# Block 1's rows as SyncE's first load, and its raw transposes ahead of V of block 0

## The chip, the cores and the metric

The kernel runs on one core of a Trainium2 chip. The metric is the device time of one execution in microseconds (us). Before the change the median of three runs is 236.48 us (236.21 to 236.73).

## What is computed

Two branches work on the same normalised input of 2048 rows by 512 columns, and are added to it: A is an attention of 32 heads over a sliding, dilated window of 8 positions, B is a gated MLP in which the positions are mixed by a 2048 by 2048 matrix.

```python
xn = layernorm(x)                              # x: [2048, 512]
# A: q, k, v = xn @ wqkv; 32 heads of 16; window of 8 positions, step 2
q, k, v = split(xn @ wqkv)
attn = softmax(mask(q . k[s - 2*w], w = 0..7) * 16**-0.5)
A = (sum_w attn[w] * v[s - 2*w]) @ wo
# B: gated MLP, gate mixed over the positions
z = gelu(xn @ w_in)                            # [2048, 1792]
z1, z2 = z[:, :896], layernorm(z[:, 896:])
B = (z1 * (w_sp @ z2 + b_sp[:, None])) @ w_out
out = x + A + B
```

## The kernel before

The 2048 rows are worked on in 16 blocks of 128 rows and 4 groups of 512. All inputs are bfloat16. For a matmul the rows of x must lie along the free dimension, so each block is transposed. Blocks 1 to 15 are normalised on VectorE and then transposed by a DMA that SyncE issues (`xTd1` and so on, L640). Block 0's normalised rows are transposed on TensorE instead (`xTr0`).

V, the product of x with the last third of `wqkv`, is wanted early to give TensorE work. For blocks 0 to 2 (`NRAW = 3`) it is therefore computed from raw rows, before the layernorm's statistics are known, and mended later (L754). These raw rows are transposed on TensorE as products with an identity (`pe_tr`, L600): block 0 in two tasks of two 128-column matmuls each (`xTx0a`, `xTx0b`), blocks 1 and 2 in one task of four (`xTx1`, `xTx2`). ScalarE copies the result out of PSUM (L628): for blocks 0 and 1 in two halves (`xTc0_0`, `xTc0_1`, `xTc1_0`, `xTc1_1`), for block 2 in one piece. V of a block is two tasks of two 512-column matmuls (L700): `V0_0` takes the first half of the transposed block and of V's weights (`ldwv0`), `V0_1` the second half of both (`ldwv1`). Then come `z2` (L831, x with the second half of `w_in`), Q and K (L723), `z1` (L877), the mixing matmul (L977), and the output (L1033, L1042).

Until the first rows have landed TensorE runs warm-up matmuls on a constant (L581): `warm0` to `warm5` with 512 columns, `warm6` with 128, and one more of 128 columns, `warm7`, between block 0's transposes and V.

Order. Each operation is a task with the tiles that it reads and writes. A planner (`Plan.schedule`) places the tasks by estimated durations and so fixes the order on every engine and the PSUM bank of every product; `emit` then writes the instructions in this order with the semaphore waits that the tiles ask for. A bank that is handed out again makes its new user wait for the old one's readers. Two things are given to the planner by hand: lists of names that must follow one another (L1073 to L1083), among them TensorE's order of the first 11 us, and the landing times of the early loads (`land`, L1089), in ns. In the planner's order SyncE issues its loads in the order of the program text: V's weights in two halves, then rows of blocks 2 and 3, `w_in`'s second half in two parts, and rows of block 4. The rows of blocks 0 and 1 are issued by ScalarE.

What orders work around the change:

- ScalarE's queue: the loads of blocks 0 and 1, then a table load and one activation (L585), then `xTc0_0`.
- SyncE's queue: the loads above, then from `xTd1` on DMA transposes, which wait for VectorE's normalised blocks.
- VectorE: statistics of block 0 (`bnst0`, L620), small operations, statistics of block 1, and so on, in a list by hand.
- TensorE: the list by hand.

Of the kernel before, what the change touches and what calls it, by code (L numbers as in the profile page):

```python
# [346 lines left out]
def build_kernel(nc, A_x, A_wqkv, A_wo, B_x, B_w_in, B_w_sp, B_b_sp, B_w_out, out, report=False, emit=True):  # L347
# [13 lines left out]
    NWARM = 7  # L361
# [49 lines left out]
    with ExitStack() as es:  # L411
# [5 lines left out]
        def A(name, n, o2_=0):  # L417
            return ar[:, off[name] + o2_: off[name] + o2_ + n]
# [13 lines left out]
        def P(bk, n, o_=0):  # L432
            return ps[:, bk.col(o_): bk.col(o_) + n]
# [78 lines left out]
        def dma(eng, fn, nbytes, chan, reads=(), writes=(), name="", xbar=False, prio=0.0, after=()):  # L512
            return T(eng, fn, reads=reads, writes=writes, name=name, prio=prio, after=after,
                     dma=dict(chan=chan, nbytes=nbytes, xbar=xbar, iss=(1270.0 if nbytes < 400000 else 2200.0) if xbar else None))
# [18 lines left out]
        def ld_x(b, eng="sp"):  # L533
            sl = b
            return dma(eng, lambda e: e.dma_start(A("xin", 512, 512 * sl), x2[128 * b:128 * b + 128, :]), 128 * 512 * 2,
                ("xin", sl), writes=[("xin", sl)], name="ldx%d" % b)

        def ld_wv(hf):
            dma("sp", lambda e: e.dma_start(AC(off["wv"] + 1024 * hf, [[512, 2], [1, 512]]),
                                            A_wqkv[256 * hf:256 * hf + 256, 1024:1536].rearrange("(c p) n -> p c n",  # L540
                                                                                               p=128)),
                256 * 512 * 2, ("wv", hf), writes=[("wv", hf)], name="ldwv%d" % hf)
# [13 lines left out]
        def ld_wqk(which, eng):  # L556
# [4 lines left out]

        dma("act", lambda e: e.dma_start(A("xin", 512), x2[0:128, :]), 128 * 512 * 2, ("xin", 0),
            writes=[("xin0", 0), ("xin0", 1)], name="ldx0")
        ld_x(1, "act")
        ld_wv(0)
        ld_wv(1)
        ld_x(2, "sp")
# [8 lines left out]
        ld_wqk(1, "sp")  # L576

        bw = plan.bank("warm")
        for wi in range(NWARM + 1):
            n_ = 512 if wi < 6 else 128  # L580
            T("pe", (lambda bw, n_: lambda t: t.matmul(P(bw, n_), ones[:, 0:128], ones[:, 0:n_], start=True,  # L581
                                                       stop=True))(bw, n_),
              writes=[bw], est=(427.0 if n_ == 512 else 107.0), name="warm%d" % wi, prio=1000)
# [487 lines left out]

        byname = {t.name: t for t in plan.tasks}
        for names in (["warm%d" % wi for wi in range(NWARM)] +  # L1073
                      ["xTx0a", "xTx0b", "warm%d" % NWARM, "V0_0", "xTx1", "V0_1", "xTx2", "V1_0", "V1_1", "xTr0", "V2_0", "V2_1",
                       "z2_0_0", "z2_0_0b", "z2_0_1", "z2_1_0", "z2_1_1", "z2_2_0", "z2_2_1", "V3_0", "V3_1", "z2_3_0", "z2_3_1", "V4_0", "V4_1", "z2_4_0", "z2_4_1", "Q0_0", "Q0_1", "K0_0", "K0_1"],
                      ("rstd7", "Vw3"),
                      ("bnst0", "bnag0", "vpe0", "bnst1", "bnag1", "vpe1", "norm0", "bnst2", "norm1", "bnag2", "vpe2", "bnst3", "norm2",
                       "bnag3", "vpe3", "norm3", "bnst4", "bnag4", "vpe4", "mr", "norm4", "bnst5"),
                      ["bnst%d" % b for b in range(5, NB)],
                      ("xTc0_0", "xTc0_1", "xTc1_0", "xTc1_1", "xTc2_0", "xTe0_0", "xTe0_2", "Ve1", "Ve0", "Ve2",  # L1080
                       "z2g0", "z2g1", "z2s0"), ("ldx4", "xTd1", "xTd2", "xTd3", "xTd4", "ldq", "ldk", "ldx5", "ldx6", "ldx7", "ldwin1", "ldx8"), ("ldx15", "xTd5"),
                      *[("ldwin1", "ldx%d" % b) for b in range(9, NB)], *[("z2_4_1", "%s0_%d" % (n, c)) for n in "QK" for c in range(4)],
                      ("V10_1", "Q3_3"), ("csa", "csb", "csc", "csr", "ldwout"), ("csr", "ldwo0"), ("csr", "ldxr0"), ("csv", "zr3")):  # L1083
            for n0, n1 in zip(names, names[1:]):
                if byname[n0] not in byname[n1].deps:
                    byname[n1].odeps.add(byname[n0])

        plan.schedule(tol=4.0, dma_bw=285.0, dma_lat=1600.0, overlap=60.0,
                      land=dict(ldx0=3600.0, ldwv0=4120.0, ldx1=4550.0, ldwv1=5230.0, ldx2=5600.0, ldwin2a=7650.0, ldx3=6050.0,  # L1089
                                ldwin2b=8950.0, csa=75800.0, csb=78400.0, csc=83400.0, csr=86500.0, ldx4=9100.0, ldx5=18150.0, ldq=16300.0, xTd3=12130.0, ldk=17800.0, ldx6=18500.0, ldx7=18900.0, xTd4=13900.0, xTd1=9600.0, xTd2=10850.0, ldwin1=21500.0))  # L1090
        if report:
            print("arena", AR, "fp", FR)
# [17 lines left out]
def bass_parallel_sum__sliding_local_dilated__mixer_gmlp__prompt_kernel(  # L1110
    nc, A_x, A_wqkv, A_wo, B_x, B_w_in, B_w_sp, B_b_sp, B_w_out, out
):
    build_kernel(nc, A_x, A_wqkv, A_wo, B_x, B_w_in, B_w_sp, B_b_sp, B_w_out, out)
# [28 lines left out]
```

## Time and profile before

| | us |
|---|---|
| median of 3 runs | 236.48 (236.21 to 236.73) |
| the profiled execution | 236.54 |
| its span in the profile | 235.3 |
| VectorE busy | 207.3 (88%) |
| ScalarE busy | 95.9 (41%) |
| GpSimd busy | 29.4 (12%) |

The span is the time from the program's first instruction to its last on the core; some 1.2 us of the execution lie around it. Times inside the profile count from the span's start. A matmul's row in the profile shows it from its start to the modelled end of its last result, and the next one starts before that end, so the distance of two starts tells the rate. Weight loads (PEld) run beside the matmuls. The chain of waits is followed back from the last instruction: at each step to what released it, or to the instruction before it on its engine.

### The profile page before, as it was taken

The page shows a single profiled execution, that of the slowest core. Times are in us where ns is not written, and L with a number is a line of the kernel's source. Part 1 is how long each engine was busy: PE and PEld are TensorE (multiplying, and loading weights), DVE is VectorE, ACT ScalarE, POOL GpSimd, SP SyncE. Part 2 cuts the span into 40 slices and gives each one's busy share as a digit, 9 for nine tenths or more (in the row PEclk, how much of TensorE's full clock was granted, in tenths as well). Part 3 has the DMA queues.
Part 4 walks back from the last instruction along what each step waited for, and adds up shares of the span by engine and source line. Part 5 has one row for each costly group of instructions (what it writes and reads, how often), then busy time and mean ns, then how long its engine had stood idle before and what let it go on. Part 6 is the DMA issues. An engine that isn't in the chain of part 4 may idle for free.

```text
span 235.3 us, 3002 instructions
## 1 busy us (share of the span) xinstructions
PE 232.4 (99%) x1127; PEld 109.0 (46%) x1127; DVE 207.3 (88%) x271; ACT 95.9 (41%) x143; POOL 29.4 (12%) x58
## 2 busy tenths in 40 slices
PE   8999999999999999999999999999999999999996
PEld 3545445544454444444444444444444444444443
DVE  4706899999999999999899999998899998999723
ACT  3788878888986679610120531111111111000000
POOL 2305740404361202000000000000000000000000
PEclk9999999999999999999999999999999999999999
DMA  6669934999911285346199999999969849945442
GB/s 221 203 193 368 181 68 103 215 202 214 228 45 50 67 231 173 66 94 175 58 353 239 273 212 266 195 236 288 279 180 306 269 145 303 288 115 156 111 137 68
DMA packets 83991, 44.55 MB, mean 189 GB/s; under 512 B 56180, under 2 KB 83204, under 8 KB 83976
## 3 DMA queue, kind: packets, MB, share of 16 engines
q1 hardware_dynamic: 82744, 41.94, 69.6%
q0 software_dynamic: 800, 2.11, 3.0%
q10 hardware_dynamic: 432, 0.30, 0.4%
q8 instruction: 9, 0.15, 0.3%
q14 instruction: 6, 0.05, 0.1%
HBM read 26.62 MB, written 4.22 MB: 131 GB/s over the span
## 4 chain that ended last, share of the span: by engine, by line
PE 98%; DVE 0%; ACT 0%; issue 0%; DVEq 0%
PE ps L977 41%; PE ps L723 12%; PE ps L831 10%; PE ps L877 10%; PE ps L1042 10%; PE ps L700 6%; PE ps L1033 6%; PE ps L581 1%; PE ps L767 1%; PE ps L600 1%; DVE arena L1048 0%; ACT arena L628 0%; PE ps L778 0%; DVEq L325 0%
## 5 line engine op out<-in xcount | busy, mean ns | idle before, releaser
L977 PE MATMUL ps<-arena 128*128 128x512 bf16 x448 | 97.0, 379 | 0.0
L977 PEld LDWEIGHTS ps<-arena 128*128 128x128 bf16 x448 | 43.8, 98 | 53.0 <-issue 0.4
L985 ACT ACTIVATE arena<-ps 128x1024 bf16<-128x1024 f32 (+1 forms) x16 | 14.7, 917 | 77.0 <-PE ps L977 70.6
L1005 DVE TENSOR_TENSOR arena<-arena 128x4096 bf16<-128x4096 bf16 x16 | 36.4, 2282 | 0.0
L744 DVE TENSOR_TENSOR arena<-arena 128x4096 bf16<-128x4096 bf16 x16 | 36.4, 2280 | 0.0
L1008 DVE TENSOR_TENSOR arena<-arena 128x2048 bf16<-128x2048 bf16 (+1 forms) x32 | 30.0, 948 | 0.2
L723 PE MATMUL ps<-arena 128*128 128x512 bf16 x128 | 28.8, 379 | 0.0
L749 DVE TENSOR_TENSOR arena<-arena 128x4096 bf16<-128x4096 bf16 x12 | 27.4, 2287 | 0.1
L1042 PE MATMUL ps<-arena 128*128 128x512 bf16 (+2 forms) x119 | 27.0, 366 | 0.0
L831 PE MATMUL ps<-arena 128*128 128x448 bf16 x128 | 25.5, 352 | 0.0
L877 PE MATMUL ps<-arena 128*128 128x512 bf16 x112 | 24.5, 379 | 0.0
L723 PEld LDWEIGHTS ps<-arena 128*128 128x128 bf16 x128 | 14.4, 113 | 13.3 <-ACT arena L713 0.4
L732 ACT ACTIVATE arena<-ps 128x1024 bf16<-128x1024 f32 x16 | 16.2, 1022 | 6.8 <-PE ps L723 6.6
L1048 DVE TENSOR_TENSOR arena<-ps,arena 128x512 bf16<-128x512 f32 (+2 forms) x17 | 11.2, 656 | 8.6 <-PE ps L1042 8.5
L831 PEld LDWEIGHTS ps<-arena 128*128 128x128 bf16 x128 | 12.5, 98 | 12.1 <-issue 0.2
L1042 PEld LDWEIGHTS ps<-arena 128*128 128x128 bf16 x119 | 11.4, 98 | 12.9
L877 PEld LDWEIGHTS ps<-arena 128*128 128x128 bf16 x112 | 11.0, 98 | 13.2
L700 PE MATMUL ps<-arena 128*128 128x512 bf16 x64 | 16.8, 395 | 0.2 <-ACT arena L628 0.2
L1033 PE MATMUL ps<-arena 128*128 128x512 bf16 (+2 forms) x68 | 16.6, 366 | 0.0
L839 ACT ACTIVATE arena<-ps 128x896 bf16<-128x896 f32 x16 | 14.6, 913 | 3.4 <-PE ps L831 3.3
L883 ACT ACTIVATE arena<-ps 128x1024 bf16<-128x1024 f32 (+1 forms) x16 | 14.0, 919 | 4.4 <-PE ps L877 4.3
L620 DVE BATCH_NORM_STATS2 fpool<-arena 128x6 f32<-128x512 bf16 x16 | 10.7, 685 | 5.5 <-DMA arena<-in_A_x_dram 5.5
(64 smaller groups left out, 168.2 us busy)
## 6 DMA issues: line engine op xcount, KB each, us to landing
arena<-vscr SPq DMA_DIRECT2D x16, 1024.0 KB, 6.1
arena<-in_A_x_dram SPq DMA_DIRECT2D x30, 128.0 KB, 3.8
vscr<-arena POOLq DMA_DIRECT2D x16, 128.0 KB, 3.9
out_dram<-arena SPq DMA_DIRECT2D x15, 128.0 KB, 2.0
arena<-in_A_wqkv_dram SPq DMA_DIRECT2D x2, 512.0 KB, 4.6
arena<-in_B_w_in_dram SPq DMA_DIRECT2D x2, 448.0 KB, 4.9
arena<-in_B_w_in_dram SPq DMA_DIRECT2D x1, 896.0 KB, 8.2
arena<-in_B_w_out_dram SPq DMA_DIRECT2D x1, 896.0 KB, 5.9
```

Source lines behind the costliest of these rows:

```text
L700: last = t.matmul(P(bk, 512), A("xcT", 128, 512 * b + 128 * dc) if b < NRAW else xTv(b, dc), A("wv", 512, 512 * dc), start=(dc == 0), stop ...
L723: last = t.matmul(P(bk, 512, 512 * which), AC(off["wqk"] + 2048 * which + 512 * dc + c, [[4, 128]]), AC(off["xnT"] + dc * S + 512 * j, [[1 ...
L732: T("act", lambda a: a.activation(AC(qo, [[ko - qo, 2], [1, 512]]), P(bk, 1024).rearrange("p (t n) -> p t n", t=2), ACTF.Copy, scale=0.5), ...
L744: T("dve", (lambda pbv, qb, kb: lambda v: v.tensor_tensor(pbv, qb, kb, ALU.mult))(pbv, qb, kb), reads=rd, writes=[("pb", s_)], est=c_tt(40 ...
L749: T("dve", (lambda av, bv: lambda v: v.tensor_tensor(av, av, bv, ALU.add))(av, bv), reads=[("pb", 1)], writes=[("pb", acc)], est=c_tt(4096 ...
L831: last = t.matmul(P(bk, 448, 512 * hf), xTv(b, dc), AC(off["w_in2"] + 896 * dc + 448 * hf, [[1, 448]]), start=(dc == 0), stop=(dc == 3))
L877: last = t.matmul(P(bk, 512, 512 * i), AC(off["w_in1"] + 896 * dc + 128 * fc, [[1, 128]]), AC(off["xnT"] + dc * S + 512 * j, [[1, 512]]), ...
L977: last = t.matmul(P(bk, 512, 512 * i), AC(off["z2"] + FH * sh + 128 * fc, [[1, 128]]), AC(off["wT%d" % r_] + sh * 512, [[1, 512]]), start= ...
L1005: T("dve", lambda v: v.tensor_tensor(tv, tv, av, ALU.mult), reads=[("attn", b)], writes=[("Vs", sv)], est=c_tt(4096), name="pv%d" % b, pri ...
L1008: T("dve", (lambda n: lambda v: v.tensor_tensor(A("Vs", n, 4096 * sv), A("Vs", n, 4096 * sv), A("Vs", n, 4096 * sv + n), ALU.add))(n), wri ...
L1033: last = t.matmul(P(bk, cn), AC(off["OT"] + 512 * tb + 128 * cc, [[1, 128]]), AC(off["wo"] + 512 * cc + c0, [[1, cn]]), start=(cc == 0), s ...
L1042: last = t.matmul(P(bk, cn), AC(off["z1T"] + fc * S + 128 * tb, [[1, 128]]), AC(off["w_out"] + 512 * fc + c0, [[1, cn]]), start=False, sto ...
```

## The change

Three edits and the planner's dates that go with them:

- The load of block 1's rows goes from ScalarE's queue to SyncE's. As it stands in the text ahead of `ldwv0`, it becomes SyncE's first load.
- `warm7` is left out.
- In TensorE's list, `xTx1` moves ahead of `V0_0`, directly behind block 0's transposes. The order was `xTx0a, xTx0b, warm7, V0_0, xTx1, V0_1`; it becomes `xTx0a, xTx0b, xTx1, V0_0, V0_1`.
- `land` has new dates for `ldwv0` (4400 for 4120) and `ldx1` (3850 for 4550).

```diff
         dma("act", lambda e: e.dma_start(A("xin", 512), x2[0:128, :]), 128 * 512 * 2, ("xin", 0),
             writes=[("xin0", 0), ("xin0", 1)], name="ldx0")
-        ld_x(1, "act")
+        ld_x(1, "sp")
         ld_wv(0)
         ld_wv(1)
         ld_x(2, "sp")
...
-        for wi in range(NWARM + 1):
+        for wi in range(NWARM):
...
         for names in (["warm%d" % wi for wi in range(NWARM)] +
-                      ["xTx0a", "xTx0b", "warm%d" % NWARM, "V0_0", "xTx1", "V0_1", "xTx2", "V1_0", "V1_1", "xTr0", "V2_0", "V2_1",
+                      ["xTx0a", "xTx0b", "xTx1", "V0_0", "V0_1", "xTx2", "V1_0", "V1_1", "xTr0", "V2_0", "V2_1",
...
-                      land=dict(ldx0=3600.0, ldwv0=4120.0, ldx1=4550.0, ldwv1=5230.0, ldx2=5600.0, ldwin2a=7650.0, ldx3=6050.0,
+                      land=dict(ldx0=3600.0, ldwv0=4400.0, ldx1=3850.0, ldwv1=5230.0, ldx2=5600.0, ldwin2a=7650.0, ldx3=6050.0,
```

## The prediction

> **What bounds the kernel now.** I read the page's first part first, then the chain of waits in order of time for the first 16 us, then the issues of the early loads one by one with their landings, then the bytes moved per microsecond.
>
> ```profile
> PE 232.4 (99%) x1127; PEld 109.0 (46%) x1127; DVE 207.3 (88%) x271; ACT 95.9 (41%) x143; POOL 29.4 (12%) x58
> ```
>
> TensorE is the bound: 232.4 of 235.3 us. So the change is worth what it takes out of TensorE's stream, or puts in. The chain shows where that stream still has holes (start, length, what):
>
> ```profile
> 0.84 2.83 PE ps L581 x7
> 3.66 0.37 PE ps L600 x2
> 4.03 0.02 issue
> 4.05 0.39 ACT arena L628
> 4.44 0.04 issue
> 4.49 1.04 PE ps L700 x2
> 5.53 0.43 PE ps L600 x4
> 5.95 0.85 PE ps L700 x2
> 6.81 0.29 PE ps L600 x4
> 7.10 0.86 PE ps L700 x4
> 7.96 0.22 PE ps L600 x4
> 8.18 0.86 PE ps L700 x4
> ```
>
> L581 is the warm-up, L600 the raw transposes, L700 V. Two things are to be seen. At 4.05 the chain leaves TensorE for 0.45 us: V of block 0 waits for ScalarE's copy (L628) of block 0's first transposed half, and only `warm7` fills 0.1 of it. And the rate doubles near 6.8 us: four 128-column transposes take 0.43 at 5.53 (0.107 each) and 0.22 at 7.96 (0.055 each); two 512-column matmuls take 0.85 at 5.95 (0.427 each) and four take 0.86 at 7.10 (0.215 each). The trace's record of the granted clock begins at 6.82. So whatever is moved out of the time before 6.82 is worth half of itself afterwards.
>
> The early loads (operation, KB each, us from issue to landing): first the two issued at 0.80 and 0.81, then those at 1.31 and 1.25, then the one at 1.82.
>
> ```profile
> arena<-in_A_wqkv_dram SPq DMA_DIRECT2D x1, 256.0 KB, 3.3
> arena<-in_A_x_dram ACTq DMA_DIRECT2D x1, 128.0 KB, 2.8
> ...
> arena<-in_A_wqkv_dram SPq DMA_DIRECT2D x1, 256.0 KB, 3.9
> arena<-in_A_x_dram ACTq DMA_DIRECT2D x1, 128.0 KB, 3.3
> ...
> arena<-in_A_x_dram SPq DMA_DIRECT2D x1, 128.0 KB, 3.8
> ```
>
> With the trace's two decimals they land: x0 3.57, wv0 4.11, x1 4.53, wv1 5.23, x2 5.60, x3 6.07. What moved meanwhile (last column, GB/s, that is KB per us):
>
> ```profile
> 1.00:2.00 1.00, 1.00 (x3) 0.29 (x2) 0.19 (x1) 0.26 (x1) 0.33 (x3) 1.00 0.12 27
> 2.00:3.00 1.00, 1.00 (x4) 0.37 (x3) 0.00 (x0) 1.00 (x1) 0.00 (x0) 1.00 0.73 217
> 3.00:4.00 1.00, 1.00 (x7) 0.46 (x6) 0.40 (x1) 0.23 (x2) 0.00 (x0) 1.00 1.09 379
> 4.00:5.00 1.00, 0.84 (x6) 0.31 (x4) 0.93 (x4) 0.66 (x2) 0.15 (x1) 1.00 1.06 372
> ```
>
> From 3 us on the DMA engines are full (share 1.06 to 1.09), so a landing follows from how many bytes stand ahead of it, not from the queue it is in. Summed up, 244 KB have moved by 3.0 and 623 KB by 4.0. The set x0, wv0, x1 (524 KB) is through at 3.74 and its last member lands at 4.53; with wv1 (786 KB) 4.44 and 5.23; with x2 (917 KB) 4.79 and 5.60. The lag is 0.8 us each time.
>
> **The change part by part.**
>
> *Loads.* x1 leaves ScalarE's queue and becomes SyncE's first load. Every later SyncE load is issued one slot (about 0.5 us, from issues at 0.80, 1.31, 1.82, 2.32, 2.79, 3.27, 3.82) later: wv0 at 1.31, wv1 1.82, x2 2.32, x3 2.79, w_in2a 3.27, w_in2b 3.82, x4 4.32. SyncE's next work is the DMA transpose of block 1 at 6.96, which waits for VectorE, so 2 us of cover lie behind the last. By bytes: x0 and x1 (262 KB) are through at 3.05, so x1 lands at 3.85; bounds 3.57 (x0's row, a load of that size issued at that time) and 4.11 (wv0's row, today's first SyncE load). wv0 is the last of 524 KB: 4.53 at the latest by bytes, 4.11 as today at the earliest; its own lag was shorter than x1's, so I take 4.45. wv1 closes the same 786 KB: 5.23 as before; late bound, the whole slot, 5.74. x2 and x3 likewise stay, or come up to 0.5 later: VectorE takes up x2 at 5.94 (0.3 cover) and x3 at 7.13 (1.0), w_in2b lands at 8.52 for a matmul at 9.64, x4 at 8.86 for 9.56. ScalarE is free 0.46 us sooner, for its table load (1.74 to 3.02) only; its next work comes at 4.05: nothing.
>
> *VectorE.* Block 1's statistics start at 4.61, 0.07 after the small operation at 4.54 began, the same step as from 5.54 to 5.62 further on: VectorE's order sets it, not x1. Gain nothing, loss nothing up to x1 at 4.55.
>
> *TensorE, in starts.* Block 0's transposes run 3.62 to 4.02 as now. Then, in place of `warm7` (0.107) and 0.363 idle, the four transposes of block 1: 4 x 0.107, 4.02 to 4.45 (x1 at 3.85 is in time; if it comes at 4.11 they run 4.16 to 4.59). V's first half needs ScalarE's copy, which ended at 4.43 and gave the start at 4.49, and wv0: with 4.45 it starts at 4.50; with 4.53, 4.58. It takes 0.83 (4.49 to 5.32 now). The second half needs wv1 at 5.23 + 0.05, so starts at 5.33 rather than 5.745; its copy ended at 4.71. The cover of 0.51 that wv1 had is down to 0.05: this is what is late next. Net: 0.415 us at the slow clock (0.427 moved into the hole, less 0.01).
>
> *What that is worth at the end.* Now the first V matmul of block 1 starts at 6.934. After: second half of V0 to 6.18, x2's transposes to 6.61, that first V matmul at 6.61, 0.21 of it at the slow clock and 0.11 at the full one, the second at 6.93. So one full-clock 512-column matmul less from there on: 0.21 us.
>
> *Is it carried to the end?* After that the stream waits nowhere. I compared each TensorE step with the end of what it needs: the shortest leads are 0.28 (block 0's z2, on L608's copy) and 0.29 (V2, on block 2's copy), and both copies follow TensorE and so move with it; from 10 us on no lead is below 0.43, and those short ones are evictions that follow TensorE too. Block 1's DMA transpose lands at 9.50, needed at 10.40. The last VectorE additions and stores follow the last matmul.
>
> *The planner.* It fixes the orders by its own estimates; there V0's second half waits for wv1 (due 5.23 in both), so all later starts come out the same. Banks change names: xTx1 takes V0's former bank and V0 takes xTx1's, and the first z2 still gets the pair of warm-up and xTx0a. I cost it at nothing.
>
> Sum: 236.54 (the profiled execution: span 235.3 and 1.2 around it) - 0.21 = 236.33; against the median of 236.48, 236.27. **I predict 236.3 us**, 0.09% less, under the 0.2% (0.47 us) that a measurement of this kernel tells from no change. Its own range: 236.48 - 0.22 (nothing late) to 236.48 - 0.12 (wv0 and wv1 0.15 to 0.2 late), with the 0.26 by which the runs shown stray to each side: 236.0 to 236.6.
>
> **The rivals.**
>
> *The weights slip a slot.* For it: the issue does come 0.5 later, and the cover at wv1 is gone. Then wv1 lands at 5.74, V0's second half starts at 5.80, 0.05 later than now: 236.5. Against: the bytes ahead of it are the same and the engines are full.
>
> *The full clock comes at another moment.* The row: it came at 6.82, after 6 us of matmuls with holes of 0.16 and 0.36. Were it not tied to the kernel's start, each us sooner would save 0.5 and each us later cost 0.5, until data stop it: with full rate at 4.3, V0's second half still waits for wv1 (5.33 to 5.76), x2's transposes end 5.98, four V matmuls 6.85, where the forecast has 7.57; the z2 matmul that follows meets block 1's transpose at 9.55, which takes 0.15 back: 236.27 - 0.57 = 235.7. At 7.6 it would be 236.27 + 0.39 = 236.66. Against: the runs before stray by 0.52 in all, where this would give over 1.5. The Trainium skill ("TensorE: Matmul & The Clock Gate", Part 1: The HAM clock gate) says that the gate opens after a busy window of about 3.4 us which runs freely and isn't reset by the kernel. By that rule the time would lie anywhere from 235.7 to 236.7; the one trace here can't show it.
>
> *Slower: a bank.* If the planner gives the first z2 the pair in which V0 lies, z2 (8.67 after the gain) waits for ScalarE's copy of V0 out of the bank, the second L707 of three, 9.34 to 10.04: start 10.09, 1.42 lost, 236.27 + 1.42 = 237.7. It decides once that copy ends after 8.6. For it: V0 does change banks. Against: by the planner's rule (the free pair that came free first) warm-up's and xTx0a's pair wins, free since 4.5.
>
> **How the numbers follow.** Forecast 0.58; slip 0.14; clock sooner 0.13 and later 0.07; bank 0.05; anything else 0.03, to either side. Faster by over 0.2%: clock sooner, and some 0.06 of the forecast's strays: 0.19. Slower by over 0.2%: bank, a third of clock later, a share of the rest and of strays: 0.11. Same: 0.70. The range takes the forecast, the slip, and most of the clock's both sides: 235.7 to 236.8.
>
> **What would show it.** Right: no ScalarE piece in the chain at 4.05; eight L600 in a row from 3.62; L700 at 4.5, its third at 5.3; first V of block 1 at 6.6; the clock's record still at 6.8. Wrong: SyncE's first x load landing after 4.1; V's second half after 5.5; a weight load of L831 waiting for L707; the full rate at another time than 6.8.

## The result and the profile after

The changed kernel is slower. Over 22 runs of each on one chip the medians are 237.14 us (236.39 to 238.86) after and 236.21 us (235.76 to 236.85) before; the ratio is 1.005, with a 95% interval from 1.0032 to 1.0068. The forecast was 236.3 us in a range up to 236.8. The profiled execution of the changed kernel took 237.29 us, with a span of 236.0, so 0.75 us more than the profiled one before.

The 22 times do not lie in one heap. Fifteen run from 236.39 to 237.50 (middle one 236.78), seven from 238.21 to 238.86 (middle one 238.47), and nothing lies between. The kernel before has no such second heap.

The page's first part, and from its list of costliest groups the line of V's matmuls and that of z2's weight loads (the last field is the idle time ahead of them, and what ended most of it):

```profile
PE 231.6 (98%) x1126; PEld 108.3 (46%) x1126; DVE 207.2 (88%) x271; ACT 95.8 (41%) x143; POOL 29.5 (13%) x58
...
L700 PE MATMUL ps<-arena 128*128 128x512 bf16 x64 | 15.9, 379 | 1.6 <-DMA arena<-in_A_wqkv_dram 1.0
...
L831 PEld LDWEIGHTS ps<-arena 128*128 128x128 bf16 x128 | 12.4, 98 | 12.7 <-DMA arena<-in_B_w_in_dram 0.6
```

TensorE works 0.8 us less and yet the span is 0.7 longer: it idles 4.4 us now and idled 2.9 before. V's matmuls wait 1.0 us for V's weights. The chain of waits of the first 12 us (start, length, what) no longer runs along TensorE:

```profile
0.80 0.39 SPq L535
1.19 0.06 issue
1.26 0.41 SPq L539
1.67 0.05 issue
1.72 0.46 SPq L539
2.18 0.04 issue
2.22 4.68 DMA arena<-in_A_x_dram
6.90 0.02 issue
6.92 0.69 DVE fpool L620
7.62 0.31 DVE arena L646
7.93 0.03 DVE fpool L622
7.96 3.12 DMA arena<-arena
11.08 0.05 issue
11.13 0.93 PE ps L831 x4
```

It is SyncE's three issues, then the load of block 2's rows, which takes 4.68 us from its issue to 6.90, then the statistics of block 2, the normalisation of block 1 and its DMA transpose, which lands at 11.08 and which z2 waits for. Block 1's normalisation stands in this chain because VectorE's hand-written list puts block 2's statistics ahead of it. In the kernel before this load landed at 5.60 and the transpose at 9.50.

TensorE's timeline of the changed kernel (start, length, engine, line, count; in brackets the idle time before and what ended it):

```profile
3.52 0.85 PE L600 MATMUL ps<-arena 128*128 128x128 bf16 x8
4.95 0.59 PE L700 MATMUL ps<-arena 128*128 128x512 bf16 x2 [0.58 <-ACT arena L628]
6.58 0.61 PE L700 MATMUL ps<-arena 128*128 128x512 bf16 x2 [1.03 <-DMA arena<-in_A_wqkv_dram]
7.02 0.39 PE L600 MATMUL ps<-arena 128*128 128x128 bf16 x4
7.24 1.03 PE L700 MATMUL ps<-arena 128*128 128x512 bf16 x4
```

All eight raw transposes stand in a row from 3.52, as meant. Then V's first half starts at 4.95, which is 0.13 after its weights' landing at 4.82 (the bracket names a copy of ScalarE's that ended then; but the copy that V's first half reads had ended at 4.34, and in e2 below, the same program with these weights down at 4.26, it starts at 4.49, so it is the weights that came last), and its second half at 6.58, right behind the other weights. Four L700 with 512 columns take 1.03 from 7.24 on, the full rate; the record of the granted clock begins at 4.04 in this execution, where before's begins at 6.82.

The loads, in the order of their issue (0.80 and 0.81, 1.26, 1.72, 2.22, and then the two parts of `w_in`), with KB and us to landing:

```profile
arena<-in_A_x_dram SPq DMA_DIRECT2D x1, 128.0 KB, 2.5
arena<-in_A_x_dram ACTq DMA_DIRECT2D x1, 128.0 KB, 2.7
arena<-in_A_wqkv_dram SPq DMA_DIRECT2D x1, 256.0 KB, 3.6
arena<-in_A_wqkv_dram SPq DMA_DIRECT2D x1, 256.0 KB, 4.8
arena<-in_A_x_dram SPq DMA_DIRECT2D x1, 128.0 KB, 4.7
```

x1 is down at 3.30 and x0 at 3.48, both in time. But wv0 lands at 4.82 (forecast 4.45), wv1 at 6.53 (forecast 5.23), x2 at 6.90 (5.60 before), x3 at 7.24 (6.07), and the two parts of `w_in` at 8.84 and 10.03 (7.26 and 8.52). The bytes moved per microsecond (last column) show the same:

```profile
3.00:4.00 1.00, 1.00 (x8) 0.56 (x7) 0.50 (x1) 0.05 (x1) 0.00 (x0) 1.00 0.80 258
4.00:5.00 1.00, 0.42 (x7) 0.27 (x5) 0.93 (x4) 1.00 (x4) 0.32 (x1) 1.00 0.89 250
5.00:6.00 1.00, 0.55 (x2) 0.05 (x2) 0.86 (x4) 0.16 (x1) 0.57 (x2) 1.00 0.74 234
```

From 258 to 234 KB per us, where the kernel before moved 379, 372 and 346, while the DMA engines are busy for 0.74 to 0.89 of the time. In the second profile of each kernel (e1 and e2 below) the difference in these three microseconds is smaller: 371, 349 and 273 before, 317, 233 and 303 after.

**Where the 0.74 us lies.** V of block 3 (L700) starts at 13.42 before and at 14.16 after; behind it both kernels need the same time to the end of the span (221.9 and 221.8). So in these two executions all of the difference is made in the first 14 us. From TensorE's first transpose to V of block 3, by distances of starts: holes after are 0.75 ahead of V's first half, 1.19 ahead of its second, 0.13 and 0.28 in z2, 2.35 in all; before they are 0.36, and `warm7` for 0.11, 0.47 in all. That is 1.88 more. The clock gives 1.11 back: before, 2.73 us of matmuls ran at half rate and lost 1.37; after, 0.52 us, which lost 0.26. The first transpose came 0.10 sooner. Net 1.88 - 1.11 - 0.10 = 0.67, against 0.74 seen.

### The profile page after: what moved, and what is told of

The parts are those of the page before. It is cut to its first block, busy times and chain, and to the rows that moved or that the text cites. A ratio compares the mean times of both kernels' runs of the same rounds, so it can differ in the third digit from the quotient of the medians.

```text
span 236.0 us, 3000 instructions
## 1 busy us (share of the span) xinstructions
PE 231.6 (98%) x1126; PEld 108.3 (46%) x1126; DVE 207.2 (88%) x271; ACT 95.8 (41%) x143; POOL 29.5 (13%) x58
## 4 chain that ended last, share of the span: by engine, by line
PE 94%; DMA 3%; DVE 1%; SPq 1%; issue 0%
PE ps L977 41%; PE ps L723 12%; PE ps L1042 10%; PE ps L877 10%; PE ps L831 10%; PE ps L1033 6%; PE ps L700 5%; DMA arena<-in_A_x_dram 2%; DMA arena<-arena 1%; PE ps L767 1%; SPq L539 0%; DVE fpool L620 0%; SPq L535 0%; DVE arena L646 0%; DVE arena L1048 0%
## 5 line engine op out<-in xcount | busy, mean ns | idle before, releaser
L700 PE MATMUL ps<-arena 128*128 128x512 bf16 x64 | 15.9, 379 | 1.6 <-DMA arena<-in_A_wqkv_dram 1.0
```

The lines of the kernel that those rows point to most:

```text
L700: last = t.matmul(P(bk, 512), A("xcT", 128, 512 * b + 128 * dc) if b < NRAW else xTv(b, dc), A("wv", 512, 512 * dc), start=(dc == 0), stop ...
```

## The experiments

The ratio is the kernel's time to that of the kernel before, run in the same job; wv1 and w_in2b are the landings, in the profiled execution, of the second half of V's weights and of the second part of `w_in`; "clock" is where the record of the full clock begins or, with "about", where the distances of the matmuls' starts halve.

| run | edit | median, us (runs) | before, us | ratio, 95% | wv1 | w_in2b | clock |
|---|---|---|---|---|---|---|---|
| e1 | none (before) | 236.19 (11) | 236.05 | 1.0004 [0.9996, 1.0013] | 5.18 | 9.10 | about 5.5 |
| e2 | the whole change | 237.36 (12) | 236.05 | 1.0052 [1.0034, 1.0071] | 6.37 | 9.49 | 4.9 to 6.4 |
| e3 | order on TensorE alone | 236.02 (12) | 236.05 | 1.0018 [0.9995, 1.0041] | 5.14 | 8.65 | about 5.7 |
| e4 | x1's queue alone | 237.32 (6) | 236.05 | 1.0055 [1.0037, 1.0074] | 5.46 | 9.68 | about 5.6 |
| e5 | before, a 16 KB load ahead | 237.07 (6) | 235.98 | 1.0056 [1.0037, 1.0075] | 5.50 | 9.43 | 4.09 |
| e6 | after, x2 by ScalarE | 236.38 (11) | 235.98 | 1.0027 [1.0011, 1.0042] | 6.19 | 8.96 | 3.76 |
| e7 | after, wv0 by ScalarE | 238.22 (6) | 235.98 | 1.0094 [1.0061, 1.0127] | 4.82 | 9.51 | about 10.1 |
| e8 | after, holes filled | 237.65 (6) | 235.98 | 1.0069 [1.0057, 1.0081] | 6.29 | 10.37 | about 6.4 |
| e9 | before, short warm-up | 237.41 (6) | 236.15 | 1.0055 [1.0037, 1.0074] | 5.29 | 8.58 | 8.35 |
| e10 | before, warm-up to the brim | 235.94 (12) | 236.15 | 0.9994 [0.9984, 1.0004] | 5.21 | 8.80 | about 4.7 |
| e11 | before, x2 by ScalarE | 236.57 (13) | 236.15 | 1.0015 [1.0006, 1.0025] | 6.12 | 9.08 | 9.87 |
| e12 | before, x1 second on SyncE | 236.81 (12) | 236.15 | 1.0036 [1.0020, 1.0051] | 6.01 | 9.42 | 4.64 |
| e13 | order alone, hole filled | 236.12 (11) | 236.03 | 1.0005 [0.9997, 1.0014] | 5.37 | 8.81 | about 6.2 |
| e14 | before, V0's second half late | 236.80 (6) | 236.03 | 1.0029 [1.0017, 1.0041] | 5.36 | 9.04 | 4.43 |

Three things were in question, one after the other: whether the loads or the order on TensorE made the loss; why the loads came late, through the issue slot that each of SyncE's loads is put back, or through a second queue that runs empty early; and how a late load turns into time, through the idle alone or also through the clock. Where an expectation shortens a theory to a letter or a name, the reading below it says in words what became of it.

### Noise, and the change in its two halves: e1 to e4

e1 is the kernel before once more, without an edit.

> The kernel before once more. Theory L (the new order of the loads slows all early loads): V's second weight half lands at 5.2 as in its first trace, the times lie between 235.7 and 236.9 with none above 237.2. Theory D (one disturbed execution): landings of this kernel stray by a microsecond as well. Theory C (the full clock comes at a window's end that isn't tied to the kernel's start): the record of the granted clock begins at another moment than 6.82, and the time moves by half of the difference.

It sets the scale: 1.0004, and single times from 235.71 to 236.50. In its profiled execution the full rate came at about 5.5, some 1.4 us sooner than in the first one, and yet the time is only 0.25 us less (236.29 against 236.54): z2 now waits for the second part of `w_in`, which landed at 9.10, and then for block 1's transpose, 0.44 us in all. So in the kernel before an early clock is largely taken back by these waits.

e2 is the changed kernel once more, without an edit.

> The changed kernel once more. Theory L: x1 lands near 3.3, V's weights near 4.8 and 6.5, the core moves some 250 KB per us from 3 to 7 us as in its first trace, against 370 before. Theory D: the landings are those of before within 0.5 us (5.2 to 5.7 for the second half). Theory C: two heaps of times, 236.4 to 237.5 and 238.2 to 238.9, some 1.7 apart, half of a window of 3.4 us; in the upper heap the clock record begins after 7 us.

1.0052: the loss holds in another job, and so does the lateness of wv1 (6.37, with V's second half 1.53 behind the matmul before it). wv0 was in time here, at 4.26 where 4.8 was expected, and the bytes moved at 317, 233, 303 and 318 KB per us from 3 to 7 us where some 250 were expected. Two of its twelve times lie above 238, and four from 237.52 to 237.73, where the 22 runs had nothing: the gap between the heaps is narrower than those showed.

e3 is the changed kernel with the load of x1 given back to ScalarE, so that only the order on TensorE and the missing `warm7` differ from before:

```diff
-        ld_x(1, "sp")
+        ld_x(1, "act")
```

> The order on TensorE alone (xTx1 ahead of V0_0, no warm7), block 1's rows still on ScalarE's queue. xTx1 then waits for x1 at 4.53, V0_0 starts near 5.0, V0_1 near 5.8, 0.1 later than before. Theory L: landings as before (5.2 for wv1), time within 0.15 of before. A theory that the order on TensorE makes the loss: 0.7 or more slower.

Ten of the twelve times lie from 235.61 to 236.29, as before; two, 238.28 and 238.50, stand alone. Its timeline:

```profile
4.46 0.61 PE L600 MATMUL ps<-arena 128*128 128x128 bf16 x4 [0.31 <-DMA arena<-in_A_x_dram]
4.86 1.43 PE L700 MATMUL ps<-arena 128*128 128x512 bf16 x4
```

x1's transposes wait for x1, so 0.52 us (from 3.95) are empty, and V runs without a break behind them. In the ten the order makes neither a gain nor the loss; the two others carry the interval up to 1.0041, and e13 below has the order without such times.

e4 is the other half: the kernel before with x1's load on SyncE's queue, and `warm7` and TensorE's order as before.

```diff
-        ld_x(1, "act")
+        ld_x(1, "sp")
```

> The queue alone (block 1's rows as SyncE's first load), TensorE's order and warm7 as before. Theory L: wv0 near 4.8, wv1 near 6.5, x2 near 6.9; V0_0 near 4.9 and V0_1 near 6.6; 0.6 to 0.9 slower than before, with an upper heap too. The theory that TensorE's order makes the loss: within 0.2 of before.

1.0055, as much as the whole change. So the loss belongs to the move of the load. Here the weights came earlier than expected (wv0 at 4.37 for 4.8, wv1 at 5.46 for 6.5), and the loss shows further on; from the view of waits between 3 and 14 us (who, for whom, us in total, times, longest):

```profile
PEld ps L831 <- DMA arena<-in_B_w_in_dram: 1.3, 2, 0.7
...
PEld ps L831 <- DMA arena<-arena: 0.5, 1, 0.5
PE ps L700 <- DMA arena<-in_A_wqkv_dram: 0.3, 1, 0.3
PE ps L831 <- DMA arena<-in_B_w_in_dram: 0.3, 1, 0.3
```

z2 waits for both parts of `w_in`, which landed at 8.44 and 9.68, for block 1's transpose, and V for wv0. Which of the loads strays furthest differs from one profiled execution to the next.

### Why the loads come late: e5, e6, e7, e11, e12

e5 leaves x1 on ScalarE's queue and puts another load ahead of V's weights on SyncE's: 16 KB, into a buffer that isn't in use yet. Every later issue of SyncE is put back as in the change, with almost no bytes added.

```diff
-        ld_wv(0)
+        dma("sp", lambda e: e.dma_start(A("Za", 512)[0:16, :], x2[0:16, :]), 16 * 512 * 2, "dummy", writes=["Za"], name="lddummy"); ld_wv(0)
```

> The kernel before with one tiny load (16 rows, 16 KB, into a scratch tile) as SyncE's first, so that every other SyncE load is issued one slot later as in the changed kernel, while blocks 0 and 1 stay on ScalarE's queue. Theory S (the slot): V's weights, x2, x3 and w_in land 0.5 to 1.3 later than before (5.7 to 6.5 for wv1), 0.4 to 1.2 slower. Theory R (the empty second queue): with 256 KB on ScalarE's queue the landings are those of before (wv1 5.2 to 5.3), time within 0.2 of before.

```profile
4.98 0.59 PE L700 MATMUL ps<-arena 128*128 128x512 bf16 x2 [0.79 <-DMA arena<-in_A_wqkv_dram]
```

1.0056, again the whole loss, without x1 moved: V's first half waits 0.79 us for wv0, which landed at 4.85, and `w_in`'s second part comes at 9.43. wv1, at 5.50, strayed less than the theory of the slot had it (5.7 to 6.5). The two queues keep their loads here, so an early empty second queue isn't needed for it.

e6 is the changed kernel with x2 on ScalarE's queue (`ld_x(2, "act")`), which gives the queues two x loads and the rest, as before, and takes the slot away for all loads behind x2.

> The changed kernel with block 2's rows on ScalarE's queue, so that this queue again holds two loads (256 KB) and SyncE's loads from x3 on are issued when they were before; wv0 and wv1 stay one slot late. Theory R: DMA rate from 3 to 7 us back at 340 to 370 KB per us, wv1 near 5.2, x2 near 4.7, w_in2b near 8.6; time 0.1 to 0.3 below before, no upper heap. Theory S: wv1 still 5.5 to 6.5, the later loads as before; 0.2 to 0.8 slower than before.

1.0027: about half of the loss is gone by the middle of its interval, which overlaps with the change's; w_in2b is back at 8.96, but wv1, whose slot stays late, lands at 6.19. This fits the slot; that a filled second queue would bring wv1 back does not.

e7 is the changed kernel with wv0 on ScalarE's queue instead (`ld_wv(0, "act")`), so that wv1 gets its old slot.

> The changed kernel with the first half of V's weights as ScalarE's second load: queue ACT x0, wv0 (384 KB), queue SP x1, wv1, x2 and so on, each SyncE load from wv1 on issued when it was before. Theory R and theory S agree here: wv0 near 4.5, wv1 near 5.2, the rate back at 340 to 370; V0_0 at 4.5 to 4.6, V0_1 at 5.3; 0.1 to 0.3 below before. If it is as slow as the changed kernel, then x1 ahead of the weights does it by itself.

wv1 did come early, at 4.82, but wv0 only at 5.24, and V's first half, which needs it, was later than in any other run, at 5.37 (as in the changed kernel, the bracket names a copy that it doesn't need):

```profile
5.37 1.87 PE L700 MATMUL ps<-arena 128*128 128x512 bf16 x4 [0.71 <-ACT arena L628]
7.46 1.91 PE L700 MATMUL ps<-arena 128*128 128x512 bf16 x4
9.17 0.63 PE L600 MATMUL ps<-arena 128*128 128x128 bf16 x4
```

The expectation was missed, and by something that neither theory of the loads held: the matmuls are still at half rate at 9 us (four take 1.9, where the changed kernel's took 1.03). Five of its six times are above 238, and one is 236.38. The clock had to be taken into the account.

e11 is the kernel before with x2 on ScalarE's queue (`ld_x(2, "act")`): x1, wv0 and wv1 keep their slots and all SyncE loads behind them are issued sooner.

> The kernel before with block 2's rows as ScalarE's third load, so that SyncE's loads from x3 on are issued one slot sooner; bytes and total are the same. Theory S (a SyncE load's landing follows its issue): w_in2b lands 0.4 to 0.6 sooner (8.0 to 8.6), V's weights as before. Theory B (bytes alone): w_in2b 8.5 to 9.1 as before. Time within 0.2 of before in both.

wv1 lands at 6.12 although it was issued as early as before. So the issue slot isn't the whole cause either, and the expectation by it was missed. But the profiled execution is the slowest of the thirteen, 238.27, with the clock at 9.87. The other twelve lose only 0.16% on average; where wv1 landed in them isn't known.

e12 is the kernel before with x1 as SyncE's second load, behind wv0 (`ld_wv(0)` first, then `ld_x(1, "sp")`).

> Block 1's rows as SyncE's second load, behind the first half of V's weights; TensorE's order and warm7 as before. Theory S: wv0 at 4.1 as before, so no hole ahead of V0_0; wv1 and all later loads a slot late (wv1 5.5 to 6.5, w_in2b 9.2 to 10.0): 0.1 to 0.6 slower, with little or no upper heap, since V0_0 comes in time. Theory that x1 on SyncE's queue slows all loads: wv0 late too (4.4 or later), 0.5 or more slower with an upper heap.

wv0 is early (4.01), wv1 late again (6.01), and the ratio is 1.0036. Every layout of the loads but before's own has something late in its one profile, the changed kernel in both of its two.

What is late about these loads can be seen in the trace. Each load's semaphore goes up sixteen times, and a wait is for the sixteenth. For wv1 the moments of some of these steps were (us):

```
                 1st    8th   12th   14th   15th   16th
before           4.62   4.89   5.14   5.15   5.20   5.23
e1 (before)      4.66   4.87   5.13   5.14   5.17   5.18
after            4.65   5.23   5.59   6.17   6.38   6.53
e2 (after)       4.50   4.84   5.71   5.73   5.76   6.37
e4               4.57   4.77   4.94   5.00   5.12   5.46
e11              4.59   4.97   5.04   5.12   5.14   6.12
e12              4.42   4.92   5.02   5.87   5.90   6.01
```

The first eight steps come at 4.8 to 5.2 in every one, as the sum of the bytes says. The last ones make the difference: more than 0.5 us behind the eighth comes one step in e4 and in e11, and three to five in the changed kernel, e2 and e12. The Trainium skill ("DMA: Bandwidth & Descriptors", Why a DMA increments its semaphore by 16 and not by 1) has it that a DMA runs on up to 16 engines that finish independently and that only the full count means landed; the trace agrees. It seems that an engine falls back through single packets: most packets of these loads take 41 or 46 ns, but some take 0.3 to 0.96 us, and the lateness stays in the loads that follow (in e2 the 16th step is 0.6 us behind the 15th for wv1, x2 and x3 alike). That these are packets of the same engine is a reading; the trace doesn't name a packet's engine. Between 2.9 and 8.4 us there are 0 to 4 such packets over 0.3 us in each of the seven profiles with before's loads (before, e1, e3, e9, e10, e13, e14), and 5 to 23 in each of the nine profiles with other ones (the changed kernel has two). Why the one order of loads has them and the other not stayed open.

### What late loads cost, and the clock: e8, e9, e10, e13, e14

e9 is the kernel before with a shorter warm-up, so that TensorE is empty for 0.73 us ahead of the first transposes (0.93 by distances of starts), while the loads stay as they are. The planner's durations for the warm-up were changed with it; the order on the other engines is the same.

```diff
-    NWARM = 7
+    NWARM = 5
...
-            n_ = 512 if wi < 6 else 128
+            n_ = 512 if wi < 4 else 128
```

> The kernel before with two 512-column warm-up matmuls fewer, so that TensorE is idle from 2.6 to 3.6 us; loads and all else as before. Theory C (a freely running window of 3.4 us opens the clock only if it is busy enough): windows that hold this idle time fail, so the full clock comes between 6.8 and 10.3, 2 to 3 us later on average: median 237.0 to 237.7, a spread of about 1.7, landings as before (wv1 5.2). Theory that only loads make slow runs: within 0.15 of before, since nothing waits for the warm-up.

1.0055, with the loads in time (wv1 at 5.29). Its timeline:

```profile
3.54 0.61 PE L600 MATMUL ps<-arena 128*128 128x128 bf16 x4 [0.73 <-DMA arena<-in_A_x_dram]
...
7.02 1.69 PE L700 MATMUL ps<-arena 128*128 128x512 bf16 x4
8.54 0.39 PE L600 MATMUL ps<-arena 128*128 128x128 bf16 x4
```

The empty time lies ahead of all useful work, so by itself it costs nothing; but the record of the full clock begins at 8.35, and V's four matmuls of block 1 still take 1.69. That is 1.53 us later than in before's first profile, and the time is 0.79 us longer (237.33 against 236.54), about half of that. So this hole on TensorE is paid through the clock.

e10 goes the other way, the warm-up's last two pieces grown to 256 and 448 columns:

```diff
-            n_ = 512 if wi < 6 else 128
+            n_ = 512 if wi < 6 else (256 if wi == 6 else 448)
```

> The kernel before with its two holes filled: warm6 with 256 columns for 128, warm7 with 448 for 128. Theory C: fewer windows fail, the full clock comes up to 0.5 us sooner on average, 0.1 to 0.25 faster than before, none slower than the slowest of before. Without the gate: the same within 0.1, or up to 0.1 slower where the filler ends after the data.

0.9994, not told from no change: to fill before's hole of 0.36 us gained nothing that could be measured.

e8 is the changed kernel with its two holes filled by constant matmuls of 512 columns (L584), one ahead of V's first half and three ahead of the second:

```diff
-                      ["xTx0a", "xTx0b", "xTx1", "V0_0", "V0_1", "xTx2", ...
+                      ["xTx0a", "xTx0b", "xTx1", "fill0", "V0_0", "fill1", "fill2", "fill3", "V0_1", "xTx2", ...
```

> The changed kernel with one 512-column warm-up matmul ahead of V0_0 and three ahead of V0_1, in the holes that the late weights leave. It computes the same. Theory C (a window of 3.4 us that is busy enough opens the clock, and the holes fail it): no time above 237.8, where the changed kernel has a quarter of its runs above 238.2; lower heap as it was or up to 0.3 higher. Theory without the gate (loads alone make the spread): the upper heap stays in a quarter of the runs.

```profile
4.42 0.63 PE L584 MATMUL ps<-const-bfloat16-1.0 128*128 128x512 bf16 x1
...
5.71 1.18 PE L584 MATMUL ps<-const-bfloat16-1.0 128*128 128x512 bf16 x3
6.72 0.59 PE L700 MATMUL ps<-arena 128*128 128x512 bf16 x2
```

There is one heap, from 237.09 to 237.81, but it isn't where the lower one was expected: it lies 1.67 above before, where the changed kernel's lower heap lies 0.57 above. The profiled execution had the latest w_in2b of all, 10.37, and the last filler held V's second half to 6.72 though wv1 was down at 6.29. And six runs can't show that seven in 22 have become none (by chance alone six without one come up about one time in ten). So this run settles nothing about the heaps.

e13 does the same to e3's half: TensorE's new order with before's loads, `warm7` kept with 448 columns in the hole ahead of `xTx1`.

> TensorE's new order (xTx1 ahead of V0_0) with block 1's rows on ScalarE's queue, and with warm6 of 256 and warm7 of 448 columns, warm7 ahead of xTx1, so that the hole before x1's landing is filled. Theory C: the slow runs near 238.4 that the order alone had (two of twelve) are gone; median 235.8 to 236.1, as the other filled version. If the order were worth the 0.2 us of the prediction beside that, 235.6 to 235.8. A theory that the order itself makes slow runs: some near 238.4 again.

1.0005, 235.74 to 236.57, and no time apart. With the hole filled the new order is worth nothing that could be measured. This is the order without the early x1, though: x1 landed at 4.36 and its transposes start at 4.40, where the forecast had 4.02.

e14 leaves before's loads and makes V's second half of block 0 wait for x3, the latest of the early x loads (6.59 here), in place of a late wv1. The planner's date for x3 is set to 5230 with it; the order on every engine is that of before:

```diff
-                T("pe", mm, reads=[("xcT", b, hf) if b < NRAW else ("xnT", b), ("wv", hf)], writes=[bk],
+                T("pe", mm, reads=[("xcT", b, hf) if b < NRAW else ("xnT", b), ("wv", hf)] + ([("xin", 3)] if (b, hf) == (0, 1) else []), writes=[bk],
```

> The kernel before, whose V0_1 also waits for block 3's rows (landing 6.0 to 6.4, where wv1 lands 5.2); loads, orders and all else as before. It stands for a late second weight half alone. If late weights by way of TensorE make the loss: V0_1 at 6.1 to 6.5, 0.3 to 0.7 slower in the lower heap (236.5 to 237.0), and an upper heap of a sixth to a third of the runs near 238. If the loss needs the other loads' lateness too: within 0.2 of before.

```profile
4.98 0.40 PE L600 MATMUL ps<-arena 128*128 128x128 bf16 x4
6.72 0.59 PE L700 MATMUL ps<-arena 128*128 128x512 bf16 x2 [1.34 <-DMA arena<-in_A_x_dram]
```

One wait of 1.34 us in this place costs 0.0029 x 236 = 0.7 us of the 0.0050 x 236 = 1.2 that the change costs. None of the six times lies in an upper heap, which the expectation had for a sixth to a third of them: one hole at this place isn't enough for that, or six runs were too few. In the profiled execution the clock was up at 4.43, ahead of the hole.

## Why the prediction was wrong

**What bounds the kernel, and where it would go: right.** In the profiled pair the loss is made in TensorE's stream in the first 14 us, and nowhere else.

**Loads: the step that failed.** "From 3 us on the DMA engines are full (share 1.06 to 1.09), so a landing follows from how many bytes stand ahead of it, not from the queue it is in." x1 (3.30 against a forecast of 3.85, bounds 3.57 to 4.11) and the middle engines' part of wv1 (4.8 to 5.2 against 5.23) went by that, or better. But what the matmul waits for is the last of sixteen parts, and the sum of bytes says nothing of it. "wv1 closes the same 786 KB: 5.23 as before; late bound, the whole slot, 5.74": it was 6.53, and 6.37 in e2. The bound was taken from the issue, as if being issued half a microsecond later could cost no more than that half. In the changed kernel's first profile wv1 came 1.3 us later than before and each load behind it 1.2 to 1.6; with the load's move alone (e4) it was 0.05 to 0.2 for wv1, x2 and x3, and 1.2 for those behind. In e11's profile wv1 came 0.9 us later with no slot lost.

**The covers behind it: wrong by the same term.** x2 was given 0.3 of cover and x3 1.0; they came 1.30 and 1.17 later. "w_in2b lands at 8.52 for a matmul at 9.64" had 1.1 of cover; it landed 1.5 later, and in e4 this was where the time went. The block 1 transpose, "lands at 9.50, needed at 10.40", landed at 11.08. The list of covers was the right list; every one of them was smaller than what the loads could stray.

**VectorE: half right.** Block 1's statistics didn't depend on x1. Block 2's did on x2, and through VectorE's order the normalisation and the DMA transpose of block 1 behind them.

**TensorE: right in form, nothing in worth.** Eight L600 in a row, no ScalarE piece in the chain at 4.05. The gain of 0.21 needed V to follow at 4.50 and 5.33; it came at 4.95 and 6.58. e13, with before's loads and the hole filled, is at 1.0005 with an interval from 0.9997 to 1.0014, which leaves out a gain of 0.21 us (0.09%); but x1 comes no earlier there. No profile has an early x1 with both halves of V's weights in time, so whether the gain would come under its own conditions stays untested.

**Planner and banks: right.** No z2 weight load waited for a copy out of PSUM in the changed kernel's page, and the orders of the other engines stayed. The rival with the bank didn't come about.

**The rival "the weights slip a slot": the right place, the wrong price.** It had V's second half wait for wv1, but at 5.74 and with 0.05 us of loss (236.5). With wv1 at 6.4 to 6.5 instead, a wait like that costs 0.7 us (e14).

**The clock: wrong to hold it apart from the change.** It was priced as something that varies by itself, whatever the change, and its weight was kept down because "the runs before stray by 0.52 in all". With more runs before strays by 1.3 us (235.51 to 236.85), and the full rate came at 6.82 in one profiled execution and near 5.5 in another. What the forecast missed is that the change itself makes holes that the clock answers to. Over all sixteen profiled executions the full rate began anywhere from 3.76 to 6.82 in thirteen, and in three at 8.35 (e9), 9.87 (e11) and about 10.1 (e7), each with a hole of 0.5 to 0.9 us ahead of it. Eight of the sixteen hold a record of the full clock, and it lasts 228.69 us (before, e9, e11) or 232.11 us (the other five): 67 and 68 times 3.413. The Trainium skill ("TensorE: Matmul & The Clock Gate", Part 1: The HAM clock gate) says that the gate goes by a free-running window of 3413 ns that must be busy. The trace agrees: the records last whole numbers of such windows, the thirteen starts fit in one such width, and the three lie one width further on (3.4 us earlier they would be at 4.94, 6.46 and 6.7). 3.4 us more at half rate cost 1.7 us, and that is the distance of the changed kernel's two heaps (238.47 - 236.78 = 1.7). e9 shows the mechanism with no load moved, and the profiled executions of e7 (238.32) and e11 (238.27) show it at the times of an upper heap. For the changed kernel itself no profile fell there (in its profiled execution the clock was up at 4.04, ahead of the first hole). Of its nine times above 238, two here and one in e2 (238.74, 238.86, 238.72) have a mean granted clock of 0.993, where every other run has 1.0: that is a record of half rate over about 3.3 us, an estimate from 2 x 0.007 x 237.5. The other six show nothing, since the mean counts the time ahead of the first record as full (it stands at 1.00 from 1 us on in the kernel before); for them the clock is inferred. By the means of the 22 runs the change costs 1.18 us: 0.65 in the lower heap, and 0.53 more through the seven runs of the upper one.

**Left open.** Why single packets of a load take 0.3 to 0.96 us in some orders of the loads and hardly ever in before's. Neither the slot (e11), nor an empty second queue (e5, e6, e11), nor the bytes alone (e5) explain it, as far as one profile of each can tell. What e8's single heap owes to its fillers and what to its late `w_in` isn't separated. No version tried was shown to be faster than the kernel before: the interval of e10's 0.9994 includes 1.

## What to carry to other kernels

A load's landing is that of its slowest part: a sum of bytes gives the middle, and where the order of the loads is changed, a tuned start needs more cover than the length of one issue: here the loads strayed by up to 1.6 us. Before a load is moved to another queue, list every load behind it with its cover, since all of them move, not only the one that is traded. Empty time on TensorE in the first microseconds can cost more than its length where the clock is still to rise; look at whether the times of a kernel fall into two heaps before explaining a median, and in which of them the profiled execution lies.

## What the hardware showed unexpectedly

- One 16 KB load ahead of others on the same queue cost 0.56% [0.37, 0.75] of the whole time (e5), more than its bytes or its half microsecond of issue.
- From 3 to 6 us the same loads moved at 379, 372 and 346 KB per us in one order and at 258, 250 and 234 in another, with the DMA engines busy for 0.74 to 0.89 of the time in the second. In the repeats it was 371, 349 and 273 against 317, 233 and 303.
- The start of the full clock differed by 6.3 us between profiled executions (3.76 to about 10.1). Holes of up to 0.36 us left no time apart (before, e10); with one of 0.52 us two of twelve did (e3), and with one of 0.9 us ahead of V (4.46 to 5.37) five of six (e7). The length alone doesn't decide: with holes of 0.8 to 1.5 us none of six (e5), one of eleven (e6), none of twelve (e12) and none of six (e14) lie above 238, and in these four profiles the clock was up before the hole or 0.1 us into it.
